# Wider steps of the crossbar: key tiles of 112, more transposes by DMA, and a new instruction order in a fused attention and FFT-convolution kernel

## The chip, the cores and the metric

The kernel runs on one core of a Trainium2 chip. A time is the device time of one execution in microseconds (us), as the median of several runs; a profile is one further execution, recorded instruction by instruction. PE is the matmul engine (PEld its weight loads), DVE the vector engine, ACT the scalar engine, POOL and SP the two engines that here mainly issue DMAs. PSUM is where PE writes, in banks that DVE and ACT empty.

## The reference

Local attention with a few global keys is followed by a gated long convolution:

```python
# q, k, v: (4 batches, 8 heads, 768 positions, 64), n_global 8, n_local 96
scores = (q @ k^T) / 8
keep   = (key < 8) | (0 <= query - key < 96)
scores += -slope[head] * distance        # 96 for a global key outside the local window
a = softmax(where(keep, scores, -1e9))
x = (a @ v), heads side by side          # (4, 768, 512)
x1, x2, x3 = split(x @ w_proj)           # w_proj (512, 1536)
x2 = irfft(rfft(x2) * rfft(filter))      # over the 768 positions
out = (x1 * x2 * x3) @ w_out             # float32
```

## The kernel before

Everything is fused, in float16 inside and float32 in PSUM. The four batches are software-pipelined: while one batch goes through the convolution, the next goes through attention.

*Attention* (`attention`, L855). The keys are cut into seven tiles of 120 local keys; with the 8 global keys in the first rows each fills 128 partitions (`KL = P - NG`, `K0`). A tile meets the 216 queries that can see it (`EW`), and the tiles go in groups `GRP` of 2, 2 and 3. For a group and each of four head pairs, `scores` (L685) runs the matmuls of the two heads on the two halves of the array, ACT takes the exponential from two banks into the tile `E` (L721), and DVE multiplies it by a mask that holds the distance bias (L738); in batch 0 the bias is added by extra matmuls in place of the mask. In `E` each tile's 216 columns stand 248 apart, with zeros in the gaps. `values` (L741) multiplies `E` by the values, whose column of ones gives the softmax sum; DVE takes the reciprocal (L785) and scales into `xn` (L780, or in small pieces on ACT, L784). Output tiles also step by 120 queries.

*Transposes.* q and k are loaded with positions on partitions by POOL's DMAs (L319), which convert to float16, into single buffers `qn` and `kn`. The matmuls need them transposed into `QT` and `KT`: batches 0 to 2 do it on PE (`turned`, L672) with a copy out of PSUM by DVE or ACT (L303), batch 3 (`XB`) by DMA transposes from the SP queue (`crossed`, L660). The attention output `xn` is transposed into `xT` on PE for all batches (`transpose_x`, L801), with a copy (L303). Copies of the global rows go from SP too (`kn<-kn`, `vn<-vn`).

*The rest* (`gate` L830, `butterfly` L808, `conv` L891). `gate` multiplies `xT` by the outer two thirds of `w_proj` (L840), evacuates x1 (L307 or L309) and x3 (L849), and multiplies them (L851). `butterfly` folds `xT` by sums and differences (tiles `xab`, `xcf`, `xo`, `xr`; L816 is its first step), so that the projection (L909, tile `ab`), the forward transform (L621, tile `X`), the products with the filter's spectrum, the inverse transform (L934, tile `eo`) and the recombination (`mix`, `half`, y*g) are short. L961 is the output projection, tile `ot` its evacuation, from which SP stores.

*What sets the order.* Each step is an operation in a list, with the engines that may run it, and what it reads and writes. `ORDER`, a string at the top, fixes the sequence of all of them: `33V` is operation 33 on DVE, `87P0` is operation 87 on PE with PSUM bank 0; A is ACT, G is POOL, S is SP. So the string also chooses between DVE and ACT where both are allowed ("AV"). Each engine runs its operations in this order and waits for what each reads:

```python
def crossed(self, what, ts, buf):
    ...
    x = g.op("S", 0.5, lambda _: nc.sync.dma_start_transpose(out=o, in_=i), ...
```

Of the kernel before, what the change touches and what calls it, by code (L numbers as in the profile page):

```python
# [18 lines left out]
KL = P - NG  # L19
# [7 lines left out]
def act(n):  # L27
    return 0.06 + n / 1200.0
# [11 lines left out]
5G 33V 34A 1V 16S 0V 12V 20S 4V 41A 43A 9V 8V 39A 10A 44A 36A 6A 49A 48A 19S 37A 45A 24G 17S 18S 50G 55G 25V 11V 26G  # L40
13V 56G 40A 42A 7V i14b0 87P0 54G 28A 53G 60G 31A 85P1 61G 59G 27A 72V 62G 52G 35A 81P2 51G 57G 46A 58G 83P3 47A 88A
29V 30V 32V 90P0 63G 89A 86A 82V 38A 91V 84A 21V 114P2 115V 94P01 98P45 116P2 78A 65G 99A 64G 15V 117V 95A 92P67 112P3
113V 93A 110P2 96P45 97A 158P3 66G 111V 122P01 123A 120P67 121A 22V 68G 159V 3G 160P3 161V 14V 23S 156P2 118P45 162P3
67G 119A 124P01 261G 157V 163V 164P23 125A 166P45 100P01 165A 101V 102V 167A 105P67 170P23 171A 69G 168P01 169A 131P45
262G 263G 106V 107V 108P2 132V 133V 260G 126P67 127V 76A 103P3 104A 109V 128V 75A 134P4 221P5 74A 135V 172P01 73A 173V
259G 129P6 216P4 177P23 79A 130V 136P6 174V 175P7 178V 70G 146P0 217A 264S 179V 180P1 137P2 222A 223V 142P3 176A 218V
219V 71G 80A 271G 202V 181A 183P1 182P4 203V 220A 224V 209V 144A 141P5 210V 138A 211V 148V 205V 361P3 273G 225A 139V
140V 272G 270G 265S 188P7 185A 362A 212V 213V 151P6 266G 363P3 2A 153V 143A 364V 359P2 360V 152P6 228P3 154V 276G
365P01 190A 184V 77A 204V 279G 366A 206V 207V 371P45 198P2 277G 226V 367V 155V 297P7 368P01 214V 372A 373V 215V 208V
200A 374P45 187P6 278G 229A 274G 145V 491G 298A 288P2 375A 269G 275G 369A 289A 488G 286P7 227V 235V 236V 189V 237V  # L50
147P4 149V 238V 287A 150V 230A 231A 232A 233V 284P2 285A 312P7 292P6 313A 293A 389P5 387P2 192P7 390A 194A 193P6 195A
388V 394P45 395A 400P01 234V 391P23 392A 239V 240V 376V 299P7 300A 437P6 401A 301P4 302A 282G 268S 433P5 435P7 438V
281G 370V 397P23 398A 241V 249P6 250A 393V 434V 247P4 436V 402V 267S 382P01 494S 242P5 248A 448P67 243A 439P23 493S
440A 383V 384V 449A 396V 303P4 377P01 197P5 199A 304A 399V 408P23 441V 492G 244P6 378V 379V 305P5 409V 410V 380P4
445P01 245A 442P23 280G 381V 306A 196V 446A 450V 403P67 404V 443A 411P5 489G 587P4 499G 405V 256P01 412A 490G 385P6
257A 505G 386A 258A 591P7 588V 252P45 253A 254A 507G 406P0 447V 456P23 661P1 444V 508G 501G 662A 407V 414P0 589P4 590A
251V 307V 416A 310P5 311A 511G 290P6 424P1 457V 458V 291A 426A 459P0 423P4 425A 429P6 308V 431A 500G 451P23 665P1
418P6 255V 592A 191V 615P4 314V 315V 506G 718G 309V 322P7 452V 246A 460A 502G 420A 453V 186V 323A 617P5 719G 454P0
455A 295V 294V 296V 732G 666V 318P6 721S 413P7 616A 330P0 316P2 509G 481V 482V 484V 317A 326P1 618A 415A 663P4 428P2
201V 430V 319A 320P3 321V 324P5 483V 325A 331V 328P7 327A 419P6 329A 421V 422V 495G 472P2 730G 664A 283G 734G 466P7  # L60
# [138 lines left out]
class Fused:  # L199
    PERIOD = 40.0  # L200
    NEAR = 3
    PAIR_X = ()
    PAIR_AB = ()
    PAIR_EO = ()
    PAIR_T = (1, 2, 3)
    PAIR_M = ()
    VD = 96
    XB = (3,)
    WL = [(0, 256), (1024, 256), (256, 256), (1280, 256), (512, 512)]
    SHIFT = 0.0  # L210
    LONG = 0.6
    EW = [216, 216, 216, 216, 216, 168, 48]
# [1011 lines left out]
```

## Time and profile before

| | us |
|---|---|
| median of 3 runs | 179.61 |
| lowest, highest run | 178.33, 181.84 |
| the profiled execution | 178.0 |
| its span, first to last instruction | 176.2 |
| PE, DVE, ACT, POOL busy in it | 163.8, 156.3, 148.7, 78.2 |
| granted PE clock | 1.00 |

The span is what the views divide up; the profiled execution's time holds 1.8 us around it. Busy time of an engine counts every instant at which one of its instructions ran; for PE, whose matmuls overlap, this is not the time that the work needs at least. A group's line gives the line of the code, engine, operation, output and input tiles, shapes, count, then busy time, the mean duration of one in ns, and the idle time of the engine just before it.

### The profile page before, as it was taken

What the parts mean: (1) busy time and instruction counts of PE and PEld (TensorE: products, weight loads), DVE (VectorE), ACT (ScalarE), POOL (GpSimd) and SP (SyncE); (2) the same over time, 40 slices, a digit from 0 to 9 for tenths busy, and PEclk for the clock granted to TensorE, in tenths of its full rate; (3) what the DMA queues carried; (4) which work ended last, traced back from release to release, by engine and by line L of the source; (5) the groups of instructions that cost most, each with busy time, mean ns of one, the idle gap of its engine ahead of it and who ended that gap; (6) DMA issues with size and microseconds to landing.
All of it is one profiled execution on the core that took longest, in us unless ns stands there. A gap on an engine that the chain in (4) does not pass through costs nothing.

```text
span 176.2 us, 4332 instructions
## 1 busy us (share of the span) xinstructions
PE 163.8 (93%) x1662; PEld 100.3 (57%) x1662; DVE 156.3 (89%) x339; ACT 148.7 (84%) x294; POOL 78.2 (44%) x99
## 2 busy tenths in 40 slices
PE   5989999689999999999899999999999999989981
PEld 2547976354655767654356767444676644556530
DVE  7685569869999999999999999999999999999960
ACT  6999998949999988889989999899856855957852
POOL 7999998828999468799950000000000000000000
PEclk9999999999999999999999999999999999999999
DMA  4999999999999989999999995400031030041564
GB/s 110 184 149 140 142 173 170 196 193 154 159 155 159 149 53 106 156 167 155 130 161 169 131 96 159 179 4 0 0 118 65 0 125 0 0 180 40 192 242 186
DMA packets 98188, 22.23 MB, mean 126 GB/s; under 512 B 90879, under 2 KB 95095, under 8 KB 98167
## 3 DMA queue, kind: packets, MB, share of 16 engines
q0 software_dynamic: 82992, 12.41, 98.6%
q1 hardware_dynamic: 15175, 9.54, 23.1%
q8 instruction: 13, 0.21, 0.5%
q14 instruction: 8, 0.07, 0.1%
HBM read 25.84 MB, written 6.29 MB: 182 GB/s over the span
## 4 chain that ended last, share of the span: by engine, by line
DVE 48%; PE 15%; POOL 11%; ACT 11%; issue 7%; DMA 6%; POOLq 0%; DVEq 0%; ACTq 0%; SPq 0%
DVE E L738 6%; PE bank L961 4%; DMA kn<-in_k_dram 4%; DVE xn L780 4%; DVE y L1041 4%; POOL vn L319 4%; DVE g L851 3%; DVE y L1036 3%; PE bank L840 3%; ACT E L721 3%; POOL kn L319 2%; DVE ab L309 2%; POOL qn L319 2%; ACT g L849 2%; DVE pp L1072 2%
## 5 line engine op out<-in xcount | busy, mean ns | idle before, releaser
L840 PE MATMUL bank<-xT,w 128*128 128x384 f16 x256 | 48.5, 326 | 0.2 <-DVE x L309 0.2
L721 ACT ACTIVATE E<-bank 128x864 f16<-128x864 f32 x48 | 40.7, 900 | 4.1 <-issue 2.2
L840 PEld LDWEIGHTS <-w 128*128 128x128 f16 x256 | 23.7, 98 | 16.1 <-issue 1.4
L319 POOL DMA_DIRECT2D kn<-in_k_dram x27 | 25.1, 935 | 6.3 <-DMA g<-in_moe_filter_fft_dram 2.7
L319 POOL DMA_DIRECT2D vn<-in_v_dram x28 | 25.5, 917 | 0.8 <-PE bank L761 0.8
L961 PE MATMUL bank<-wo,y 128*128 128x512 f16 x96 | 23.9, 379 | 1.1 <-DVE y L1041 1.1
L319 POOL DMA_DIRECT2D qn<-in_q_dram x21 | 18.9, 905 | 4.0 <-PE bank L621 3.9
L738 DVE TENSOR_TENSOR E<-E,mask 128x864 f16<-128x864 f16 x36 | 20.2, 599 | 0.0
L780 DVE TENSOR_TENSOR xn<-bank,rc 128x512 f16<-128x512 f32 (+1 forms) x22 | 16.9, 774 | 0.7
L756 PE MATMUL bank<-vn,E 128*128 128x65 f16 x224 | 15.5, 193 | 0.2 <-DVE xn L780 0.2
L307 ACT ACTIVATE ot<-bank 128x512 f32<-128x512 f32 x21 | 12.6, 620 | 3.7 <-PE bank L961 3.3
L756 PEld LDWEIGHTS <-E 128*128 128x128 f16 x224 | 14.0, 97 | 2.8 <-issue 0.8
L303 ACT CAST eo<-bank 128x384 f16<-128x384 f32 x28 | 12.3, 496 | 3.8 <-PE bank L937 3.7
L761 PE MATMUL bank<-vn,E 128*128 128x65 f16 x192 | 15.3, 193 | 0.0
L707 PE MATMUL bank<-QT,KT 64*128 64x216 f16 (+2 forms) x224 | 14.4, 241 | 0.8 <-DVE ab L309 0.3
L849 ACT CAST g<-bank 128x384 f16<-128x384 f32 x28 | 13.9, 502 | 1.5 <-PE bank L840 1.2
L961 PEld LDWEIGHTS <-y 128*128 128x128 f16 x96 | 8.8, 98 | 10.1 <-DVE y L1041 2.2
L303 ACT CAST X<-bank 128x512 f16<-128x512 f32 x24 | 13.6, 607 | 0.7 <-PE bank L621 0.7
L761 PEld LDWEIGHTS <-E 128*128 128x128 f16 x192 | 13.2, 97 | 1.0 <-issue 0.8
L307 ACT ACTIVATE x<-bank 128x384 f16<-128x384 f32 x23 | 11.4, 509 | 1.8 <-PE bank L840 1.0
L707 PEld LDWEIGHTS <-KT 64*128 64x128 f16 x224 | 8.3, 94 | 7.5 <-issue 4.6
L934 PE MATMUL bank<-inv,X 128*128 128x256 f16 x64 | 11.4, 273 | 1.1 <-DVE X L1078 1.1
(148 smaller groups left out, 348.3 us busy)
## 6 DMA issues: line engine op xcount, KB each, us to landing
out_dram<-ot SPq DMA_DIRECT2D x24, 256.0 KB
vn<-in_v_dram POOLq DMA_DIRECT2D x28, 120.0 KB, 5.6
kn<-in_k_dram POOLq DMA_DIRECT2D x27, 120.0 KB, 5.8
qn<-in_q_dram POOLq DMA_DIRECT2D x21, 128.0 KB, 5.9
w<-in_moe_w_proj_dram POOLq DMA_DIRECT2D x4, 256.0 KB, 6.8
ot<-in_q_dram SPq DMA_DIRECT2D x3, 256.0 KB
g<-in_moe_filter_fft_dram POOLq DMA_DIRECT2D x1, 768.0 KB, 11.4
w<-in_moe_w_proj_dram POOLq DMA_DIRECT2D x1, 512.0 KB, 8.7
```

The costliest lines, as they stand in the source:

```text
L303: {"A": nc.scalar.copy, "V": nc.vector.tensor_copy, "G": nc.gpsimd.tensor_copy}[e](out, in_)
L307: self.nc.scalar.mul(out, in_, c)
L319: return self.g.op(eng, 0.57 + 0.00035 * nbytes[0] if eng == "G" else 0.5, lambda _: e.dma_start(dst, src), w=w, r=r, nbytes=nbytes, name= ...
L707: nc.tensor.matmul(bs[hh].f32()[:, off:off + w], self.KT[hs, hp, P * m:P * m + P], self.QT[hs, hp, KL * m:KL * m + w], start=(off == 0 and ...
L721: g.op("A", act(864), lambda _: nc.scalar.activation(eo, bs[0].two()[:, :, 0:432].rearrange("p h (m w) -> p h m w", m=2), Act.Exp, scale=s ...
L738: g.op("V", dve(864, 2), lambda _: nc.vector.tensor_mul(eo, eo, mk), r=[("mask", 2 * hp), ("mask", 2 * hp + 1)], w=[("E", hp, gi)], name=" ...
L756: nc.tensor.matmul(o[:, n, hh], ef[:, at:at + P], vt[:, t, 2 * hp + hh, 0:D + 1], start=first, stop=(t == 0), skip_group_check=True)
L761: nc.tensor.matmul(o[:, n, hh], ef[:, at:at + P], vt[:, t - 1, 2 * hp + hh, 0:D + 1], start=False, stop=True, skip_group_check=True)
L780: nc.vector.tensor_mul(to, o[:, :, :, 0:D], rc.to_broadcast([P, 2, 2 * nt, D]))
L840: nc.tensor.matmul(bk.f32()[:, 0:h], self.w[:, c, o + P * j:o + P * j + P], self.xT[:, c, h * s:h * s + h], start=(c == 0), stop=(c == 3))
L849: first = g.op("AV", {"A": act(h), "V": 0.0005}, lambda e: nc.scalar.copy(x3, pts[1].f32()[:, 0:h]) if e == "A" else None, use=[pts[1]], w ...
L961: nc.tensor.matmul(bk.f32(), y[:, c, P * t:P * t + P], self.wo[:, c, :], start=(c == 0), stop=(c == 3))
```

## The change

- **Key tiles of 112.** A key tile holds 112 local keys; rows 0 to 7 are the global keys, rows 8 to 15 are padding (zeros in k, zeros loaded once into v by two DMAs, masked in the bias). A tile meets 208 queries, the last one 96. Output tiles step by 112. Group widths in the exponential become 416, 416 and 512 per head.
- **No gaps in `E`.** The columns of a group are contiguous; the value matmul with the previous key tile takes its remaining 96 columns and writes 96 output rows.
- **Crossbar.** `XB` becomes (2, 3): q and k of batch 2 as well as 3 go by DMA transpose. For batches 2 and 3 (`XX`) the attention output goes through it too (`crossed_x`: one DMA of up to 112 partitions by 512 for each tile, seven a batch), in place of `transpose_x`. `xn` becomes one tile for this, with the four head pairs side by side.
- **Set-up.** Slopes are written by 8 wider instructions in place of 16; the fills of `E` shrink to one.
- **Order.** `ORDER` is another sequence, with other choices between DVE and ACT. `PAIR_M`, which was empty, goes.

```diff
-KL = P - NG
+KL = 112
+LO = P - KL
...
-5G 33V 34A 1V 16S 0V 12V 20S 4V 41A 43A 9V 8V 39A 10A 44A 36A 6A 49A 48A 19S 37A 45A 24G 17S 18S 50G 55G 25V 11V 26G
...
-1021S 1022P4 1023A 1016P5 1024S 1017A 1018S
+0V 15S 1V 18S 32V 10V 5G 23G 2A 39A 36A 35A 34A 33A 6V 7V 41G 16S 9V 24V 26V 44G 25G 8V 47G 37A 45G 46G 40A 51G i14b0
...
+994P7 995A 996S
...
-    PAIR_M = ()
...
-    XB = (3,)
+    XB = (2, 3)
...
-    EW = [216, 216, 216, 216, 216, 168, 48]
+    N, LAST = 208, 96
+    EW = [208] * 6 + [96]
+    GW = [416, 416, 512]
...
-    Q0 = [0, 240, 480]
-    QW = [240, 240, 288]
+    Q0 = [0, 224, 448]
+    QW = [224, 224, 320]
+    XX = (2, 3)
...
-        self.EE = t("E", [P, 4, 2, 1536])
+        self.EE = t("E", [P, 4, 2, 1376])
...
-        self.mask = t("mask", [P, H, 648])
-        self.xn = [t(f"xn{i}", [P, 2, 7, 2, D]) for i in range(2)]
+        self.mask = t("mask", [P, H, 720])
+        self.xn = t("xn", [P, 7, 4, 2, D])
...
-        g.op("V", dve(512, 2), lambda _: v.memset(self.ot[3][0:NG], 0.0), w=[("kz", 0)], bias=-4500)
-        for lo, hi in ((1, 2), (2, 7)):
-            g.op("V", dve(512 * (hi - lo), 4), lambda _, lo=lo, hi=hi: v.memset(self.kn[0:NG, lo:hi], 0.0),
-                 w=[("kz", t) for t in range(lo, hi)], bias=-4500 if lo == 1 else -3500)
-        for i in range(4):
-            et = self.E[i]
-
-            def gaps(e, et=et):
-                gap = et[:, :, 0:1488].rearrange("p h (m w) -> p h m w", m=6)[:, :, :, 216:248]
-                if e == "V":
-                    v.memset(gap, 0.0)
-                    v.memset(et[:, :, 1456:1536], 1.0)
-                    return
-                zero = self.idle[:, 0:384].rearrange("p (h m w) -> p h m w", h=2, m=6)
-                nc.scalar.copy(gap, zero)
-                nc.scalar.activation(et[:, :, 1456:1536], self.idle[:, 0:160].rearrange(
-                    "p (h w) -> p h w", h=2), Act.Copy, bias=1.0, scale=1.0)
-            g.op("AV", {"A": 0.62, "V": 0.52}, gaps, r=["idle"], w=[("E", i, c) for c in range(3)], name="gaps")
+        g.op("V", dve(512), lambda _: v.memset(self.ot[3][0:LO], 0.0), w=["kz32"], name="kz")
+        for lo, hi in ((0, 2), (2, 7)):
+            g.op("V", dve(512 * (hi - lo), 2), lambda _, lo=lo, hi=hi: v.memset(self.kn[0:LO, lo:hi], 0.0),
+                 w=[("kz", t) for t in range(lo, hi)], name="kz")
+        g.op("V", dve(256), lambda _: v.memset(self.EE[:, :, :, 1344:1376], 1.0),
+             w=[("E", i, c) for i in range(4) for c in range(3)], name="gaps")
...
-                dst = self.slope[ps, hp].rearrange("p k c -> p (k c)")
-                dst = dst[:, 0:256].rearrange("p (k c) -> p k c", k=2)
-                for k in range(2):
-                    g.op("A", {"A": 0.145}, lambda e, ps=ps, hp=hp, k=k: self.times(
-                        e, self.slope[ps, hp, k, 64 * k:64 * k + 64], self.ident[ps, ps],
-                        self.slopes[2 * hp + ps.start // 64] / self.scale),
-                        r=["ident", "slope"], w=[("slope", half, hp, k)], bias=-2950, name="slope")
+                at = 1024 + 256 * hp
+                dst = flat[ps, at:at + 384].bitcast(BF16).rearrange("p (k c) -> p k c", k=2)[:, :, 0:64]
+                g.op("A", {"A": 0.32}, lambda e, ps=ps, hp=hp, dst=dst: self.times(
+                    e, dst, self.ident[ps, None, ps].to_broadcast([64, 2, 64]),
+                    self.slopes[2 * hp + ps.start // 64] / self.scale),
+                    r=["ident", "slope"], w=[("slope", half, hp, k) for k in range(2)], name="slope")
...
-        g, nc, NL, n = self.g, self.nc, self.NL, 216
+        g, nc, NL, n = self.g, self.nc, self.NL, self.N
...
-            for lo, hi, at in ((0, n, 0), (0, n, n), (0, 168, 2 * n), (n, n + 48, 600)):
-                v.tensor_copy(wide[:, at:at + hi - lo], dg[:, lo:hi])
+            v.tensor_copy(wide[:, 0:2 * n].rearrange("p (a b) -> p a b", a=2),
+                          dg[:, None, 0:n].to_broadcast([P, 2, n]))
+            v.tensor_copy(wide[:, 2 * n:3 * n + self.LAST], dg)
...
-        g.op("V", 0.9, spread, r=["dg", "far"], w=["wide"], name="spread")
+        g.op("V", 1.35, spread, r=["dg", "far"], w=["wide"], name="spread")
...
-            g.op("A", act(648), lambda _, h=h: nc.scalar.activation(
+            g.op("A", act(720), lambda _, h=h: nc.scalar.activation(
...
-        x = g.op("S", 0.5, lambda _: nc.sync.dma_start_transpose(out=o, in_=i), nbytes=(128 * n, 1024),
+        g.op("S", 1.25, lambda _: nc.sync.dma_start_transpose(out=o, in_=i), nbytes=(128 * n, 1024),
...
-        x.svc = 2.0 * n
...
-        g.op("P", 0.555 if near else 0.19 if gi == 2 else 0.187, run, acq=bs, r=[("QT", t) for t in qt] + [
+        g.op("P", (0.54, 0.55, 0.65)[gi] if near else (0.182, 0.182, 0.222)[gi], run, acq=bs, r=[("QT", t) for t in qt] + [
...
-        eo = et[:, :, 496 * gi:496 * gi + 496].rearrange("p h (m w) -> p h m w", m=2)
-        eo = eo[:, :, :, 0:216]
-        g.op("A", act(864), lambda _: nc.scalar.activation(
-            eo, bs[0].two()[:, :, 0:432].rearrange("p h (m w) -> p h m w", m=2), Act.Exp,
-            scale=self.scale), use=bs, w=[("E", hp, gi)], table="exp", name="exp")
+        W = self.GW[gi]
+        eo = et[:, :, 416 * gi:416 * gi + W]
+        g.op("A", act(2 * W), lambda _: nc.scalar.activation(
+            eo, bs[0].two()[:, :, 0:W], Act.Exp, scale=self.scale), use=bs, w=[("E", hp, gi)],
+            table="exp", name="exp")
...
-        if (self.b, gi) in self.PAIR_M:
-            if hp % 2:
-                hs = slice(2 * hp - 2, 2 * hp + 2)
-                ep = self.EE[:, hp - 1:hp + 1].rearrange("p a h c -> p (a h) c")[
-                    :, :, 496 * gi:496 * gi + 496].rearrange("p h (m w) -> p h m w", m=2)[:, :, :, 0:216]
-                mk = self.mask[:, hs].rearrange("p h (m w) -> p h m w", m=3)
-                mk = (mk[:, :, 0:2], mk[:, :, 1:2].to_broadcast([P, 4, 2, 216]), mk[:, :, 1:3])[gi]
-                g.op("V", dve(1728, 2), lambda _: nc.vector.tensor_mul(ep, ep, mk),
-                     r=[("mask", h) for h in range(hs.start, hs.stop)], w=[("E", hp - 1, gi), ("E", hp, gi)], name="masked")
-            return
-        mk = self.mask[:, 2 * hp:2 * hp + 2].rearrange("p h (m w) -> p h m w", m=3)
-        mk = (mk[:, :, 0:2], mk[:, :, 1:2].to_broadcast([P, 2, 2, 216]), mk[:, :, 1:3])[gi]
-        g.op("V", dve(864, 2), lambda _: nc.vector.tensor_mul(eo, eo, mk),
+        mo = (0, self.N, self.N)[gi]
+        mk = self.mask[:, 2 * hp:2 * hp + 2, mo:mo + W]
+        g.op("V", dve(2 * W, 2), lambda _: nc.vector.tensor_mul(eo, eo, mk),
...
-                        at = 248 * t if t < 6 else 248 * 5 + 168
+                        at = self.N * t
...
-                            at = 248 * (t - 1) + KL
-                            nc.tensor.matmul(o[:, n, hh], ef[:, at:at + P],
+                            at = self.N * (t - 1) + KL
+                            nc.tensor.matmul(o[0:self.LAST, n, hh], ef[:, at:at + self.LAST],
...
-        vs = [("vn", slot, t) for t in range(max(0, ts[0] - 1), ts[-1] + 1)] + [("vn1", slot)] + [
+        vs = [("vn", slot, t) for t in range(max(0, ts[0] - 1), ts[-1] + 1)] + [("vn1", slot), ("vz", slot)] + [
...
-            to = self.xn[j][:, :, ts[0]:ts[0] + nt].rearrange("p i t h d -> p i (t h) d")
+            to = self.xn[:, ts[0]:ts[0] + nt, 2 * j:2 * j + 2].rearrange("p t i h d -> p i t h d")
...
-                nc.vector.tensor_mul(to, o[:, :, :, 0:D], rc.to_broadcast([P, 2, 2 * nt, D]))
+                nc.vector.tensor_mul(to, o[:, :, :, 0:D].rearrange("p i (t h) d -> p i t h d", h=2),
+                                     rc.rearrange("p i (t h) o -> p i t h o", h=2).to_broadcast([P, 2, nt, 2, D]))
...
-                    nc.scalar.mul(to[:, i, n], o[:, i, n, 0:D], rc[:, i, n])
+                    nc.scalar.mul(to[:, i, n // 2, n % 2], o[:, i, n, 0:D], rc[:, i, n])
...
-                    nc.tensor.transpose(tx[:, o:o + P], self.xn[j][:, i, t], self.ident)
+                    nc.tensor.transpose(tx[:, o:o + P], self.xn[:, t, 2 * j + i], self.ident)
...
+
+    def crossed_x(self, c, t):
+        n = min(KL, self.S - KL * t)
+        o, i = self.xT[:, :, KL * t:KL * t + n], self.xn[0:n, t].rearrange("p a h d -> p (a h d)")
+        self.g.op("S", 1.25, lambda _: self.nc.sync.dma_start_transpose(out=o, in_=i), nbytes=(n, 1024),
+                  r=[("xn", j, c) for j in range(2)], w=[("xT", j, c) for j in range(2)], name="cross")
...
-                self.transpose_x(j, c)
+                if b not in self.XX:
+                    self.transpose_x(j, c)
+            for t in self.GRP[c] if b in self.XX else ():
+                self.crossed_x(c, t)
...
-            self.g.op("V", 0.36, ones, w=[("vn1", i)], name="ones", bias=at)
+            self.g.op("V", 0.45, ones, w=[("vn1", i)], name="ones", bias=at)
...
-        for what, o, src, t, p0 in (("q", 0, self.q, 0, 0), ("k", 3, self.k, 0, NG), ("q", 1, self.q, 1, 0),
+        for i in range(2):
+            pad = self.vn[i][NG:LO].rearrange("p t h d -> p (t h d)").rearrange("p (a b) -> p a b", a=12)
+            zero = self.idle[NG:LO, None, 0:448].to_broadcast([LO - NG, 12, 448])
+            self.load("S", pad, zero, [("vz", i)], (96, 896), "vz", r=["idle", ("vn1", i)])
+        for what, o, src, t, p0 in (("q", 0, self.q, 0, 0), ("k", 3, self.k, 0, LO), ("q", 1, self.q, 1, 0),
```

## The prediction

> **What bounds the kernel now.** I read the page's first two parts, then busy time by stretch, then the groups of instructions kept apart by shape, then the SyncE queue's own timeline.
>
> ```profile
> PE 163.8 (93%) x1662; PEld 100.3 (57%) x1662; DVE 156.3 (89%) x339; ACT 148.7 (84%) x294; POOL 78.2 (44%) x99
> DVE  7685569869999999999999999999999999999960
> DMA  4999999999999989999999995400031030041564
> ```
>
> ```profile
> 0.00:40.00 40.00, 35.04 (x441) 23.07 (x442) 29.12 (x83) 34.66 (x68) 34.07 (x51) 1.00 1.69 162
> 40.00:170.00 130.00, 126.44 (x1212) 76.36 (x1210) 127.05 (x257) 112.20 (x224) 44.08 (x49) 1.00 1.11 109
> 140.00:150.00 10.00, 9.95 (x55) 5.04 (x54) 9.83 (x19) 5.75 (x13) 0.00 (x0) 1.00 0.14 55
> 170.00:176.20 6.20, 2.33 (x10) 0.90 (x10) 0.15 (x1) 1.85 (x4) 0.00 (x0) 1.00 0.65 251
> ```
>
> The columns are length, then PE, PEld, DVE, ACT and POOL busy, the clock and DMA. In the 130 us from 40 to 170 PE is busy 97%, DVE 98%, ACT 86%; together 365.7 of 390, a mean share of 93.8%. No engine alone is the bound: work taken off one is a gain only as far as the others are relieved or can take over. ACT's slack lies after 130 (5.75 of 10 at 140). Ahead of 40 loads and set-up pace the kernel; after 170 the last stores.
>
> ```profile
> L738 DVE TENSOR_TENSOR E<-E,mask 128x864 f16<-128x864 f16 x36 | 20.2, 599 | 0.0
> L780 DVE TENSOR_TENSOR xn<-bank,rc 128x512 f16<-128x512 f32 x15 | 10.3, 690 | 0.4
> L309 DVE TENSOR_SCALAR x<-bank 128x384 f16<-128x384 f32 x9 | 5.0, 551 | 0.2
> L309 DVE TENSOR_SCALAR ab<-bank 128x512 f16<-128x512 f32 x6 | 4.1, 682 | 0.0
> L307 ACT ACTIVATE ab<-bank 128x512 f16<-128x512 f32 x18 | 11.0, 622 | 1.7 <-PE bank L909 1.5
> L784 ACT ACTIVATE xn<-bank,rc 128x64 f16<-128x64 f32 x20 | 4.3, 340 | 0.2 <-DVE rc L785 0.2
> L303 ACT COPY xT<-bank 128x480 f16<-128x480 f16 x10 | 5.6, 566 | 2.3 <-PE bank L801 2.2
> L303 ACT COPY KT<-bank 128x1024 f16<-128x1024 f16 x4 | 4.1, 1031 | 0.0
> ```
>
> ```profile
> 12.45 8.41 ACT L721 ACTIVATE E<-bank 128x864 f16<-128x864 f32 x10 [0.35 <-PE bank L707]
> 30.89 2.62 DMA kn<-kn
> 99.25 0.45 PE bank L801 x8
> 137.91 0.96 DVE xab L816
> ```
>
> ```profile
> L660 SPq DMA_TRANSPOSE KT<-kn x7: 1188/1258/1879, 82.9 to 105.3; - x7
> L660 SPq DMA_TRANSPOSE QT<-qn x6: 1190/1254/1937, 85.4 to 102.0; - x6
> 85.44 4.78 SPq L660 DMA_TRANSPOSE QT<-qn  x2
> ```
>
> The last fence is the crossbar as batch 3 uses it already: 13 crossings of one 128x512 tile, 1.25 us of the SP queue each in the middle, 1.94 at most; two once took 4.78 us together. Copying the first rows of kn inside SBUF by DMA landed after 2.62 us, my nearest row for a landing.
>
> **The change, part by part.** The order names an engine for each operation by a letter, so I counted the letters of both orders by kind. Prices are busy time over count, or the slope between two sizes.
>
> *PE.* Gone are the transposes of q and k of batch 2 (13 tiles x 4) and of x in batches 2 and 3 (2 x 28): 108, at 0.45 us for eight, 6.05 us. Added are 48 score columns per head pair and batch (group widths 432, 432, 432 become 416, 416, 512) and twice that for batch 0's bias: 0.5 us at 0.42 ns a column (four 384-column matmuls take 0.65 us). Net -5.5. The value matmuls keep their number; 96 for 128 rows in some I put at nothing (they follow one another 0.03 us apart).
>
> *DVE.* Evacuations move to ACT: x1 9 to 2 (7 x 0.56 = -3.9), ab 6 to 1 (5 x 0.68 = -3.4), xn of 512 15 to 13 (-1.4), eo, g from PSUM and inv one each (-1.0). QT and KT copies of 1024 fall 5 to 3 (-1.4), xT 8 to 6 (-0.8). Added: one X copy (0.6), two mix scalings (0.7), and the mask products: 36 at 0.517 back to back (1.55 us for three) become 24 of 832 and 12 of 1024 elements, at 0.52 ns an element 19.2 for 18.6 us (0.6). The fills of the E gaps in set-up fall by 0.9, one small negation adds 0.3. Net -10.6.
>
> *ACT.* Added: x1 23 to 30 (+3.5), x3 and eo one each (+0.9), ab 18 to 23 (+3.1), xn in small pieces 20 to 36 (16 x 0.215 = +3.4), inv (+0.4), eight masks of 720 for 648 (+0.5). An exp back to back is 0.841 us (8.41 for ten); with 0.86 ns an element (from copies of 512 and 1024) 32 of 832 and 16 of 1024 make 41.7 for 40.4 (+1.3). That the exps now write without gaps I price at nothing, since these ten ran gapped at the same slope. Gone: xT 16 to 6 (-6.0), copies of 1024 5 to 2 (-3.1) and three of 512 (-1.8), mix scalings (-1.7), slopes 16 to 8 larger ones, small fills and an X copy (-3.5). Net -3.0, of which -2.5 in set-up.
>
> *SP and DMA.* 27 crossings more, 40 in all, in one queue with the stores. Their price lies between 1.25 us (the median) and 2.39 (the pair of 4.78); I take 1.25, near eleven of thirteen rows: 50 us of a queue that has some 80 between batch 2's first loads and batch 3's last values. Behind a crossing that waits on xn stand others and two copies of vn; behind the last of batch 2's x stands its butterfly. For batch 3 the new order leaves DVE six products, two sums, three gates, a y product and two ot (8.65 us by their rows) between the last xn and that butterfly, for four crossings and a landing: 4 x 1.25 + 2.62 = 7.6 us, hidden. At 2.39 each it would be 12.2, 3.5 us late. I take 0.4 us lost in all, between 0 and 12.
>
> [...]
>
> *Loads and set-up.* Tiles of 112 rows send fewer packets; descriptor work does not show it (kn of 120 rows 935 ns, qn of 128 905), so nothing, 1 us at best, on a POOL idle after 92. Set-up: its savings stand beside waits for loads; I take nothing, between -2 (batch 1's first k tile stands earlier in the queue, and 30 to 40 has 2.3 us of idle PE) and +1.
>
> *Sum.* Within 40 to 170 the three engines lose 5.5 + 10 + 0.5 = 16 us of work. At the same mean share that is 16 / 3 / 0.938 = 5.7 us; PE alone gives the same, 5.5 / 0.973. Less 0.4 for crossings: -5.3. The span goes from 176.2 to 170.9, the profiled execution's 178.0 to 172.7. The median shown is 1.6 above that execution, so the forecast is **174.3**.
>
> **Rivals.** *The relief does not come through.* The new order could leave each engine waiting for another where each now waits 2 to 3%; at a mean share of 91% in place of 93.8 the stretch takes (365.7 - 16) / 3 / 0.91 = 128.1, so only 1.9 us are won: 177.7. For it: every operation's place is new. Against it: the work is truly gone. Chance 0.23.
>
> *DVE was the bound.* The chain that ended last is 48% DVE; if it alone sets the pace, 10 / 0.977 = 10.2 us go: 169.4. Against it: PE at 97% must then work without gaps. Chance 0.12.
>
> *The crossbar queue becomes the bound* (slower). 40 crossings at 2.39 us are 95.6; begun at about 48 us (SP's first copy of batch 2's kn rows is issued at 51.11 now), the last x tile lands near 146.2 and not at 137.9, where batch 3's butterfly starts now. With the 38.3 us that follow it today the span is 184.5: 187.9 in the median's terms. It decides from about 2.1 us a crossing on, or when one queued crossing waits long for a load. For it: loads run beside batch 2's crossings all the time (the DMA row stands at 9 until slice 24) and x crossings wait for xn in order with those of batch 3's q and k. Against it: eleven of thirteen rows were short with the loads running. Chance 0.15. [...]
>
> *No relief in work and no loss*: the order gives back just what it saves, 179.6; chance 0.07.
>
> **How the numbers follow.** The forecast itself has 0.43. A measurement of this kernel tells about 2% from no change: 176.0 and 183.2 are the limits. Below 176.0 lie nearly all of the forecast, the DVE case and a little of the first rival: 0.59. Within lie the rest of that rival, the equal case and the mild end of the crossbar case: 0.28. Slower: 0.13. The range reaches from the DVE case with a us to spare, 168.5, to the limit 183.0, leaving most of the crossbar case out.
>
> **What would show it.** Right: PE some 5 us and DVE some 10 us less busy, ACT within 3 us of now, all three at the same share from 40 to the tail; 40 crossings at a median near 1.3 us; no idle time of DVE ahead of batch 3's butterfly, that of L816's line. Wrong: crossings near 2 us, PE or DVE waiting on them by name or as unexplained issue time, the SP queue still crossing at 140 us, or DVE idle although its work fell.

## The result and the profile after

| | before | after |
|---|---|---|
| median (runs) | 180.4 us (4) | 186.25 us (4) |
| lowest to highest | 178.33 to 181.84 | 185.97 to 188.02 |
| profiled span | 176.2 us | 184.4 us |
| granted PE clock in it | 1.00 | 0.952 |
| PE, DVE, ACT busy | 163.8, 156.3, 148.7 | 165.1, 145.3, 146.7 |

The kernel became slower: the ratio is 1.043, with an interval of 1.030 to 1.055. A ratio, here and below, leaves out slow runs (of before those of 181.19 and 181.84 us), so it is not the quotient of the medians. The forecast was 174.3 us and its range ended at 183.0.

The first two parts of the page after, and its DMA queues; the lines of before stand in the prediction. The columns of the queues are packets, MB, and the packets' time as a share of 16 engines' span; q0 carries POOL's loads, q1 what SP issues: stores, copies, and the transposes by DMA, which are called crossings here.

```profile
PE 165.1 (90%) x1556; PEld 102.4 (56%) x1556; DVE 145.3 (79%) x317; ACT 146.7 (80%) x295; POOL 73.2 (40%) x99
...
PE   7999399999999999989905999969999999999991
...
DVE  7664053999999999989900899859998999999940
...
PEclk9999955899999999999985999999999999999999
DMA  5999999999999999999999943646021472001376
...
q0 software_dynamic: 75952, 11.95, 92.4%
q1 hardware_dynamic: 28984, 12.98, 32.2%
```

The work fell as counted: DVE is 11.0 us less busy, ACT 2.0. PE's busy time did not fall, but part of it ran at half clock (the fives in the PEclk row), and there the same work is slower: near 25 us two value matmuls, a pair, start every 0.13 us, where a pair takes 0.077 at full clock (140.09 to 140.63 us, seven pairs). What is new are holes: PE has a slice of 3 and a slice of 0, and DVE falls to 0 at both places. The DMA row stands at 9 from the second slice to slice 23. That row looked almost the same before (9 to slice 24); the experiments below lead back to it.

The stretch for which the forecast was made (length, then PE, PEld, DVE, ACT and POOL busy, clock, DMA) and the crossings in SP's queue (duration in ns, shortest, median, longest, and first and last start):

```profile
40.00:170.00 130.00, 119.31 (x1098) 72.32 (x1096) 114.94 (x231) 108.54 (x229) 41.00 (x49) 0.97 1.20 122
```

```profile
L651 SPq DMA_TRANSPOSE KT<-kn x14: 1203/1272/2497, 57.3 to 122.4; - x14
```

```profile
L651 SPq DMA_TRANSPOSE QT<-qn x12: 1205/1260/1672, 55.0 to 116.2; - x12
```

```profile
L793 SPq DMA_TRANSPOSE xT<-xn x14: 1184/1210/2036, 104.3 to 145.8; - x14
```

The mean share of the three engines is 342.8 of 390, or 87.9%, where it was 93.8. The crossings cost the queue what they cost it before.

What the holes wait for, first from the waits of after (us in total, times, longest), then from its chain (start, length, what):

```profile
PE bank L737 <- DMA vn<-vn: 7.1, 1, 7.1
POOL kn L321 <- DMA KT<-kn: 7.0, 1, 7.0
```

```profile
14.17 8.36 DMA vn<-idle
...
71.00 8.26 DMA KT<-kn
...
86.57 4.99 DMA vn<-in_v_dram
92.06 6.85 DMA vn<-vn
```

The first hole is the fill of v's padding rows, a DMA that the new order issues at 14.17 us and that lands 8.36 us later. At 71 us a crossing of a k tile takes 8.26 us to land; POOL's next load of k needs that tile's place in `kn`, and batch 2's loads of v stand behind it in POOL's order. They come late, the copy of their global rows comes later still, and PE stands still until 99 us.

The stretches in which the clock was halved (length, then busy PE, PEld, DVE, ACT, POOL, clock, DMA):

```profile
24.00:33.00 9.00, 9.00 (x108) 7.50 (x105) 4.49 (x12) 4.93 (x8) 8.43 (x11) 0.50 1.77 162
...
96.00:102.00 6.00, 2.95 (x31) 2.26 (x32) 0.86 (x4) 0.48 (x3) 1.06 (x2) 0.50 1.83 156
```

Each follows a hole, of 3.0 and 7.1 us. So the profile offers four suspects: two transfers that stand badly in their queues, the clock, the single buffer `kn`, and the DMA engines themselves.

### The profile page after: what moved, and what is told of

Its sections match the earlier page's. It is cut to its first block, busy times and chain, and to the rows that moved or that the text cites. A ratio compares the mean times of both kernels' runs of the same rounds, so it can differ in the third digit from the quotient of the medians.

```text
span 184.4 us, 4173 instructions
## 1 busy us (share of the span) xinstructions
PE 165.1 (90%) x1556; PEld 102.4 (56%) x1556; DVE 145.3 (79%) x317; ACT 146.7 (80%) x295; POOL 73.2 (40%) x99
## 3 DMA queue, kind: packets, MB, share of 16 engines
q0 software_dynamic: 75952, 11.95, 92.4%
## 4 chain that ended last, share of the span: by engine, by line
PE 69%; DMA 16%; DVE 4%; issue 3%; POOL 3%; SPq 2%; ACT 1%; DVEq 0%; POOLq 0%
PE bank L828 15%; PE bank L900 12%; PE bank L952 8%; PE bank L612 6%; PE bank L742 6%; PE bank L737 5%; DMA vn<-idle 5%; DMA KT<-kn 4%; DMA vn<-vn 4%; PE bank L698 4%; PE bank L301 3%; DMA vn<-in_v_dram 3%; PE bank L925 2%; PE bank L662 2%; PE bank L783 2%
## 5 line engine op out<-in xcount | busy, mean ns | idle before, releaser
L712 ACT ACTIVATE E<-bank 128x832 f16<-128x832 f32 (+1 forms) x48 | 41.9, 942 | 3.6 <-PE bank L698 3.6
L737 PE MATMUL bank<-vn,E 128*128 128x65 f16 x224 | 21.3, 210 | 10.0 <-DMA vn<-vn 7.1
L737 PEld LDWEIGHTS <-E 128*128 128x128 f16 x224 | 19.7, 120 | 12.7 <-issue 8.3
L719 DVE TENSOR_TENSOR E<-E,mask 128x832 f16<-128x832 f16 (+1 forms) x36 | 21.4, 614 | 0.0
L742 PE MATMUL bank<-vn,E 128*96 128x65 f16 x192 | 21.4, 224 | 0.0
L767 DVE RECIPROCAL rc<-bank 128x8 f32<-128x8 f32 (+1 forms) x24 | 4.9, 209 | 20.3 <-PE bank L742 19.9
L742 PEld LDWEIGHTS <-E 128*96 128x96 f16 x192 | 19.8, 143 | 0.8
L309 ACT ACTIVATE ab<-bank 128x512 f16<-128x512 f32 x23 | 13.8, 635 | 4.4 <-PE bank L900 4.3
L698 PE MATMUL bank<-QT,KT 64*128 64x208 f16 (+1 forms) x224 | 14.6, 247 | 1.4 <-DMA KT<-kn 0.8
L766 ACT ACTIVATE xn<-bank,rc 128x64 f16<-128x64 f32 x36 | 7.8, 335 | 8.9 <-DVE rc L767 8.8
```

The source lines that it names most:

```text
L309: self.nc.scalar.mul(out, in_, c)
L698: nc.tensor.matmul(bs[hh].f32()[:, off:off + w], self.KT[hs, hp, P * m:P * m + P], self.QT[hs, hp, KL * m:KL * m + w], start=(off == 0 and ...
L712: g.op("A", act(2 * W), lambda _: nc.scalar.activation(eo, bs[0].two()[:, :, 0:W], Act.Exp, scale=self.scale), use=bs, w=[("E", hp, gi)], ...
L719: g.op("V", dve(2 * W, 2), lambda _: nc.vector.tensor_mul(eo, eo, mk), r=[("mask", 2 * hp), ("mask", 2 * hp + 1)], w=[("E", hp, gi)], name ...
L737: nc.tensor.matmul(o[:, n, hh], ef[:, at:at + P], vt[:, t, 2 * hp + hh, 0:D + 1], start=first, stop=(t == 0), skip_group_check=True)
L742: nc.tensor.matmul(o[0:self.LAST, n, hh], ef[:, at:at + self.LAST], vt[:, t - 1, 2 * hp + hh, 0:D + 1], start=False, stop=True, skip_group ...
```

## The experiments

The kernel before was run again beside each group of experiments, with medians between 177.95 and 178.52 us. Ratios are against those.

### Single waits taken away

**The fill of the padding ahead** (`11V` and `13S`, two places in `ORDER`):

```diff
-0V 15S 1V 18S ... 16S 9V ... 4V 11V 87P67 ... 262G 13S 148V
+0V 15S 1V 11V 18S ... 16S 13S 9V ... 4V 87P67 ... 262G 148V
```

> The changed kernel with the first zero fill of v's padding rows (vn<-idle) issued at about 3 us in place of 14.2, so that it lands long before the first value matmuls; nothing else moves. Place in the queue (theory): the 3.0 us in which PE waits for it from 19.6 on, and the half clock from 23.7 to 33.6 behind it, are gone; the clock is 1.00 until 92; 4 to 6 us less than the changed kernel, about 181. Rival, slow landings under load: v itself lands late, PE still waits 1 to 3 us there for in_v, and no more than 2 us are won. Rival, a bad order everywhere: under 1 us.

**The copy of batch 2's first global rows of v directly behind the other copy** (`487S`):

```diff
-468P6 488S 344P4 ... 661A 487S 329V
+468P6 488S 487S 344P4 ... 661A 329V
```

> The changed kernel with the copy of batch 2's global rows into the first two v tiles (vn<-vn) issued directly behind the copy into the other five, at about 77 us, in place of 92.06; nothing else moves. Place in the queue: the wait of 7.1 us from 92 on and the half clock from 95.4 to 102 are gone; 6 to 9 us less than the changed kernel, about 178 to 180. Rival, slow landings under load: the values then wait for in_v (tile 1 is issued at 86.6 and lands some 5 us later) or for a crossing, and 3 us or less are won. Rival, a bad order everywhere: under 1 us.

**Both moves**:

> Both moves together. Place in the queue: the sum of both, 11 to 14 us less than the changed kernel, 172 to 175, a clock of 1.00 throughout, and thus 2 to 5% faster than before: the forecast's 174.3 was right but for two copies in a queue. Rival, slow landings under load: 178 to 182, with PE or DVE waiting for crossings or in_v instead. Rival, a bad order everywhere: 184 or more.

**PE kept busy in both holes** by matmuls of zeros, to see whether the clock then stays up:

```diff
-91P67 ... 595P23
+i12b6 91P67 ... i30b2 595P23
```

> The changed kernel with matmuls on zeros put ahead of the two late groups of value matmuls (12 of 512 columns at 19.6 us, 30 at 92 us), which PE runs while it waits; their results are used by nobody. The waits stay, but PE is never idle there. If the granted clock falls because PE stood idle, it stays at 1.00 and 3 to 6 us are won, about 181: that is the clock's part of the loss, and the rest is the waits themselves. If the clock falls for another reason (the instructions that come then, or DMA load), the half clock is still there and nothing is won.

Measured: 185.55 us (ratio 1.040, 1.030 to 1.049), 185.61 (1.030, 1.017 to 1.043), 184.81 (1.033, 1.025 to 1.042) and 185.42 (1.038, 1.025 to 1.050). The first three took away the waits that they aimed at, the fourth the early half clock; none brought the time back, and all four intervals overlap that of the changed kernel. With both moves the waits and the chain read:

```profile
POOL kn L321 <- DMA KT<-kn: 16.1, 2, 10.0
PEld L698 <- DMA KT<-kn: 12.3, 4, 6.3
```

```profile
56.72 12.55 DMA kn<-in_k_dram
69.29 10.46 DMA KT<-kn
96.09 7.23 DMA KT<-kn
122.45 2.43 DMA KT<-kn
```

What the early fill wins by 40 us is lost again between 55 and 110 us. A load of k lands after 12.55 us (5.8 in the median of before), a crossing behind it after 10.46, another after 7.23; when the loads are over, the crossing at 122 us lands in 2.43. The theory that two transfers merely stood in the wrong place fell here. So did the early half clock as the cause: the run with busy matmuls has a clock of 1.00 from 23 to 34 us and is as slow. Its clock fell later: the PEclk row reads 5 from 78.4 to 83.0 us. PE's own row falls first, to 5 in the slice from 73.8 us, where the clock still reads 9, and the longest new wait of PE is one of 4.9 us for `KT<-kn`; so the idle time came first there.

### The buffer, or the engines behind it

**`kn` as a ring of nine tiles**, so that a load waits for the crossing two tiles further back (with both moves):

```diff
-        self.kn = t("kn", [P, 7, H, D])
+        self.kn = t("kn", [P, 9, H, D])
+    def slot(self, b, t):
+        return (7 * b + t) % 9
```

> All 40 crossings and both early moves, but kn is a ring of nine tiles in place of seven, so that a load of k waits for the crossing two tiles further back; crossings, loads, and their order are the same. Theory: POOL's waits for DMA KT<-kn fall from 16 us to under 5, the loads of batch 2 and 3 are issued some 8 us earlier, and 184.8 falls to 179 to 182. Rival 3 (not the buffers but the 16 DMA engines: the crossings get their turn late beside the loads, and PE waits on KT and QT for that): POOL's waits fall but PE's and the weight loads' waits for KT (some 21 us together by name) do not, and the time stays at 183.5 to 185.5.

Measured 185.4 us (1.038, 1.030 to 1.046). POOL's wait for `KT<-kn` is gone; PE's waits for it are shorter but remain, and one for `QT<-qn` has come (L705 is the line of the score matmuls here):

```profile
PEld L705 <- DMA KT<-kn: 8.4, 3, 5.5
PE bank L705 <- DMA KT<-kn: 7.7, 2, 5.3
POOL qn L321 <- DMA QT<-qn: 6.6, 1, 6.6
```

The loads no longer wait for k's buffer, and the crossings land no sooner (9.73 and 7.54 us in the chain, for 10.46 and 7.23). The theory of k's buffer fell as well; the rival that names the DMA engines gave the number. The buffer of q stayed as it was, and POOL now waits for it.

### Parts undone in the changed kernel

**q and k of batch 2 on PE again, in the order of after, and the same with both moves** (`XB = (3,)`; the transposes and their copies, on DVE, were put into `ORDER` by hand):

> Only batch 3's q and k cross (13 crossings); batch 2's 13 tiles are transposed on PE again and copied out by DVE (8 groups more, some 2.9 us of PE and 6 us of DVE); x of batches 2 and 3 still crosses, and the rest of the new order stands. Theory (the crossings of q and k of batch 2, which land in 5 to 10 us beside the loads, hold the single buffers kn and qn, so that POOL's loads behind them start late): POOL's wait for DMA KT<-kn before 85 us falls from 7 to 0, the last load is issued by 92 us in place of 97; the two stalls of PE at 20 and 92 us are not touched, unless the second shrinks since the loads are earlier; 186.25 becomes 181 to 184. Rival 1 (the new order or the 112-key tiles as such cost the time): 186 to 190, as PE and DVE get work back. Rival 2 (x's crossings cost it): 186 to 189.

> The same, with the fill of the padding and the copy of batch 2's global v rows moved ahead, so that neither of PE's two long stalls should be there. Theory: what was won by these two moves is no longer given back between 60 and 110 us; granted clock above 0.985, 177 to 180, against 184.8 for the two moves alone. Rivals 1 and 2: 184 to 187, with waits of PE and DVE elsewhere (rival 2: for DMA xT<-xn, more than the 1.3 us of the kernel after).

**x on PE again** (`XX = ()`, with both moves):

> The opposite half: q and k of batches 2 and 3 cross (26 crossings), x of all batches is transposed on PE again (56 transposes more, 3.2 us of PE, and 12 copies, six on DVE and six on ACT, 3.3 us each); with both early moves. Theory (q and k's crossings hold the buffers): POOL still waits some 16 us for DMA KT<-kn, and the time is 184 to 188. Rival 2 (x's crossings cost the time): POOL may wait as before but the time falls to 178 to 181.

**q and k of all batches on PE, x crossing** (`XB = ()`, with both moves):

> The kernel after with both early moves and with q and k of all batches on PE (26 tiles, 104 transposes, some 5.9 us of PE and 16 copies on DVE, some 10 us); only x of batches 2 and 3 crosses (14 crossings, begun when the loads are over). Both theories: no wait of PE for KT or QT crossings is left, the granted clock stays at 1.00, and PE's busy time is some 168 us at 94 to 95% of the span: 176 to 180. Rival (the new order or the 112-key tiles cost time by themselves): 183 or more, with the idle time in other places.

Measured: 185.61 (1.042, 1.038 to 1.047), 182.65 (1.029, 1.021 to 1.037), 191.67 (1.076, 1.072 to 1.081), 184.16 (1.034, 1.024 to 1.043). Without the 13 crossings of batch 2, and with both moves, the median is 2.2 us below that with them, although PE has 2.9 us of work back; that is the sign that the suspicion asks for, but the intervals overlap (1.021 to 1.037 and 1.025 to 1.042) and settle nothing; it lies between the theory's 177 to 180 and the rivals' 184 to 187. Taking x's crossings away made the kernel slower, above even the 184 to 188 that was expected, so they show no sign of being the culprit. But the four kernels were not as clean as meant. In the last one the clock is at 0.998 and nobody waits for a crossing, and still it takes 184 us; both theories had expected 176 to 180, and 183 or more was the mark of the rival that the new order or the 112-key tiles cost time by themselves. Its waits:

```profile
POOL kn L321 <- PE bank L662: 8.7, 2, 5.3
...
DVE QT L305 <- PE bank L662: 5.2, 8, 1.2
```

The transposes that I put in by hand make POOL and DVE wait for PE. So the runs neither bear that rival out nor remove it; the kernel with fewer loads, below, speaks to it. The next ones alter the kernel before.

### One part done alone in the kernel before

**Batch 2's q and k cross, in the places where PE transposed them:**

```diff
-    XB = (3,)
+    XB = (2, 3)
```

> The kernel before with one part of the change alone: batch 2's q and k cross (13 crossings in the places where PE transposed them), nothing else is changed; 52 transposes and 8 copies less. Theory B: the work falls by 2.9 us on PE and some 6 us on ACT and DVE, but PE's scores of batch 2 and POOL's loads of batch 3 wait for landings of 5 to 10 us beside the loads; 181 to 186, with PE's waits for KT and QT by name over 5 us. Theory A: as slow, but then with the extra crossings of the other kernel as slow too. If crossing them were free, the time would be 174 to 176.

Measured 184.07 us (1.032, 1.025 to 1.038). This one part takes away 52 transposes and eight copies and costs 5.7 us or so (3.2% of 178). Its waits:

```profile
POOL qn L319 <- DMA QT<-qn: 10.4, 1, 10.4
...
POOL kn L319 <- DMA KT<-kn: 5.4, 1, 5.4
```

Here too crossings hold buffers, and the loads move less: from 74 to 94 us q0 carried 2.06 MB and not 2.56. This run does not tell the two apart.

### Crossings that nobody waits for

**Thirteen extra crossings in the kernel before**, of tiles of QT and KT into an unused output buffer, beside the loads:

> The kernel before with 13 crossings more of a 128x512 tile, from columns of QT and KT that batch 2 has just got, into an unused output buffer: nobody waits for them and they hold no load buffer. They are issued while the loads still run (some 70 to 80 us). Theory A (crossings take so much of the 16 DMA engines from the loads that they cost time even if nobody needs them): the loads of batch 3 land some 5 us later, 178 becomes 181 to 185. Theory B (it is the late landing of crossings that someone waits for): 178 to 180, as before within its scatter; at most the 13 real crossings of batch 3 behind them in the queue start later.

Measured 195.82 us (1.084, 1.074 to 1.094), but it is no measure of contention: the crossings waited for one another's four destinations, ACT waited 16.0 us for one of them, and the copies of vn's global rows stood behind them in SP's queue, so that PE waited 18.2 us for `vn<-vn`. The next two were meant to mend this: six crossings of zeros, each with a destination of its own, where the queue is free.

```diff
+    def extra(self, n):
+        to = ...
+        self.nc.sync.dma_start_transpose(out=to.rearrange("p (a b) -> p a b", a=4), in_=self.idle)
```

**Beside the loads:**

> The kernel before with six more crossings of a 128x512 tile of zeros into output buffers that are unused then, issued at some 74.7 to 82.2 us, where its SP queue is free and the loads of batches 2 and 3 run; nobody waits for them and the queue's next crossing is due at 82.9. Theory A (a crossing takes its share of the DMA engines from the loads, near 1 us of the load stream each by the run with 13): loads land later, POOL's last load is issued some 5 us after 90.6, 178 becomes 180 to 183. Theory B (only a landing that someone waits for costs time): 177.5 to 178.7.

**After them:**

> The control: the kernel before with the same six extra crossings behind its first six stores, from some 107 us on, when the loads are over. Both theories: 177.5 to 178.7, no difference.

Measured: 183.12 us (1.024, 1.016 to 1.033) beside the loads; 179.17 (1.003, 0.998 to 1.007) after them. Here is what the two queues moved from 74 to 94 us, in the kernel before, then with the six crossings beside the loads:

```profile
q0 software_dynamic: 19341, 2.56, 200.5%
q1 hardware_dynamic: 1697, 0.51, 18.8%
```

```profile
q0 software_dynamic: 11539, 1.85, 144.2%
q1 hardware_dynamic: 3916, 1.04, 49.1%
```

In the same 20 us the loads on q0 moved 0.71 MB less (0.86 less than the control, which moved 2.71 there). At 2.56 MB in 20 us that is 5.5 to 6.7 us of the load stream, some 0.9 to 1.1 us for each crossing. In bytes it is 0.12 to 0.14 MB for each, and a tile of 128x512 float16 holds 0.13: a crossing displaced about its own size in loads. POOL's own timeline shows the same (start, length, then the idle time before it and what ended it):

```profile
85.60 0.89 POOL L328 DMA_DIRECT2D qn<-in_q_dram  x1 [1.77 <-DMA vn<-in_v_dram]
...
91.83 0.90 POOL L328 DMA_DIRECT2D vn<-in_v_dram  x1 [1.64 <-DMA vn<-in_v_dram]
```

By this view POOL now waits, 0.3 to 1.8 us each time, until earlier loads of other tiles have landed before it issues the next. Its last load is issued at 97.8 us and not at 89.7. From 105 to 115 us PE is busy 6.88 of 10 us, where it was 9.70. PE waits there for crossings of batch 3's q and then of its k, by the waits (us in total, times, longest) and the chain (start, length, what):

```profile
PE bank L716 <- DMA QT<-qn: 2.8, 1, 2.8
```

```profile
105.00 4.94 DMA KT<-kn
```

This crossing of k was issued at 95.81 us before. Both stand in SP's queue behind two crossings of q that hold it for 9.90 us from 88.81 us on (4.78 before, 2.0 of them a wait for a load of q); loads of q land there in 11.2 us in the median from 74 to 94 us, and in 5.7 before. The queue has a part of its own, too: the six took 10.8 us of it and not 7.5 (six times 1.25), so batch 3's first crossing began 4.2 us late, at 87.07 us. In the control no crossing of batch 3 stands behind the extra ones. So the pair of runs shows that crossings delay loads; how much of the 5 us came that way, and how much through SP's queue, it does not tell.

### The stream of loads made lighter

**The 14 loads of v of batches 2 and 3 left out**, in the changed kernel with both moves and all 40 crossings, and in the kernel before as a control:

```diff
-            self.load_rows(("vn", s), vt, self.v, b, t)
+            if b >= 2:
+                self.g.op("G", 0.1, lambda _: None, w=[("vn", s, t)], name="left out")
+            else:
+                self.load_rows(("vn", s), vt, self.v, b, t)
```

> The changed kernel with both early moves (184.8) and all its 40 crossings; only the 14 loads of v of batches 2 and 3 are left out (1.7 MB; batches 2 and 3 are computed with the v that lies in the buffers, so the output is not the reference's). Theory A (crossings and loads share the DMA engines, and the stream of loads and crossings together is what is late): 14 loads less are some 12 us of the stream, crossings land sooner, PE's waits for KT and QT between 55 and 110 us and POOL's waits for crossings shrink to under 5 us, and the time falls to 174 to 178. Rival (the changed kernel loses its time in the order of its instructions on PE, DVE and ACT): 182 to 185.

> The control: the kernel before without the same 14 loads. Its engines are 93 to 98% busy between 40 and 170 us, so a lighter stream of loads can win it little: 176.5 to 178. With both at that, the difference between the two kernels is the stream and no more; with the changed kernel below it by 2% or more, the work that the change saves comes out as time once the stream is light.

Measured: the changed kernel falls from 184.81 to 175.16 us (0.980, 0.973 to 0.988, so just under 2% below before), the kernel before stays at 178.4 (1.002, 0.998 to 1.007). The same loads are worth 9.7 us to the one and nothing to the other. The page of the changed kernel without them:

```profile
PE 158.6 (92%) x1556; PEld 97.8 (57%) x1556; DVE 145.4 (84%) x317; ACT 146.9 (85%) x295; POOL 61.8 (36%) x85
...
PEclk9999999999999999999999999999999999999998
```

At full clock PE is 5.2 us less busy than before, near the 5.5 of the forecast. The new order and the 112-key tiles, with all crossings, thus run below the kernel before when the loads are fewer, which speaks against the rival that they cost the time by themselves. One part of the expectation missed: POOL still waits 13.0 us for `KT<-kn`. That wait did little harm here, with 14 loads fewer behind it: the time was 175.16 us with it. Leaving the loads out lightens the DMA engines and shortens POOL's queue at once (q0 carries 10.34 MB and not 11.95, POOL is busy 61.8 us and not 73.3), so this pair shows that the stream of loads was late, and not which of the two delays it most.

### Weights of 96 columns

In the full-clock run with x alone crossing, weight loads read (count, busy, mean ns):

```profile
L737 PEld LDWEIGHTS <-E 128*128 128x128 f16 x224 | 16.6, 108 | 1.8
L742 PEld LDWEIGHTS <-E 128*96 128x96 f16 x192 | 16.4, 126 | 0.6
```

Before, both lines had 128 columns and 97 ns; the second read:

```profile
L761 PEld LDWEIGHTS <-E 128*128 128x128 f16 x192 | 13.2, 97 | 1.0 <-issue 0.8
```

There two value matmuls followed each other in 0.062 us; here a pair takes an estimated 0.0785, and 0.077 in the timeline of the changed kernel near 140 us.

**The kernel before with 96 columns:**

```diff
-                            nc.tensor.matmul(o[:, n, hh], ef[:, at:at + P],
+                            nc.tensor.matmul(o[0:96, n, hh], ef[:, at:at + 96],
```

> The kernel before, except that its value matmuls with the previous key tile (192 of them) take 96 columns of E in place of 96 and 32 zeros, as the kernel after does. If a weight load of 96 columns is slower than one of 128 (126 to 97 ns in the traces), each such pair takes 0.0785 us for 0.062, PE is 3.2 us busier, and with PE at 93% the time is 180 to 181.5 for 178; if it is free (as the prediction took it), 177.5 to 178.5.

**The x-only kernel with 128:**

> The kernel in which only x crosses, with 128 columns of E in place of 96 in the value matmuls with the previous key tile. The 32 columns more are those of the next tile's first queries, so the sums of 16 rows of each output tile contain terms that they should not; it is for the time alone. If the 96-column load is what costs: PE's busy time falls by 3 us and 184.2 becomes 181 to 182. If not: 183.5 to 184.5.

Measured: 179.24 us (1.002, 0.997 to 1.007) and 183.19 (1.029, 1.020 to 1.036; 184.16 with 96 columns). With 128 columns the second weight load is back at 98 ns, and PE is 2.1 us less busy (164.7 for 166.8) where 192 pairs by 0.0165 us make 3.2 (2.9 by the 0.015 of the timeline). In the time of the kernel before nothing of it is seen. For the x-only kernel the two intervals overlap; whether it gains is open.

## Why the prediction was wrong, point by point

**The work terms came out near.** DVE -11.0 for -10.6, ACT -2.0 for -3.0, and PE -5.2 for -5.5 where the clock was full (-4.4 against the control without the same loads, 163.0). For PE luck has a part: the 96 columns, which the prediction "put at nothing", cost some 2 us of PE, so the rest of PE's work fell by about that much more than the sum has it. POOL's issue of a k load, put at nothing as well, fell from 935 to 836 ns with the smaller tiles; no run isolates what that is worth.

**"At the same mean share" did not hold, even with light loads.** There, from 40 to 166 us, PE, DVE and ACT are busy 119.92, 116.49 and 108.81 us, a mean share of 91.3%; the control keeps 93.8% from 40 to 170. That 175.16 us lies near 174.3 is luck in part: the kernel before stood at 178.5 beside it and not at 179.6, so 3.4 us were won where the forecast had 5.3.

**The step that failed is the one under "SP and DMA".** It priced a crossing by the SP queue: 1.25 us of issue, with 2.39 as the upper bound. That price was right: the medians of after lie between 1.21 and 1.27 us. But SP was not what ran short. By the runs it was the stream of loads beside the crossings: the DMA row stands at 9 to slice 23, six added crossings took 0.71 to 0.86 MB from it in 20 us, and with 14 loads fewer the changed kernel took 175.16 us. The sum has no term for it. The row of 9s to slice 24 was quoted and served only to ask whether crossings would be issued slowly. A crossing took 0.9 to 1.1 us of the load stream in the run with six, so the 13 of batch 2 that stand beside loads are an estimated 12 to 14 us of it. From 55 to 97 us the two queues moved this, before and then after:

```profile
q0 software_dynamic: 37371, 4.96, 182.1%
q1 hardware_dynamic: 2988, 0.85, 14.1%
```

```profile
q0 software_dynamic: 28334, 4.03, 153.9%
q1 hardware_dynamic: 9424, 2.40, 46.1%
```

The loads moved 0.93 MB less there; over the whole span they are only 0.46 MB smaller (11.95 for 12.41).

**The landing was mis-sized.** 2.62 us, from a copy of `kn` rows, fits the crossings after the loads: 2.4 us for xT with both moves, issued from 99.7 to 144.6 us. Beside loads they took 7 to 10.5 us in the chains above.

**Waits that the change adds were not named.** A load of batch 3's k or q now waits until a crossing of batch 2 has landed and no longer for a transpose on PE; behind it on POOL stand the loads of v. And the fill of the padding rows, counted with set-up at nothing, took 8.36 us to land, 3.0 of them on PE's path. Moving the fill and the copy of v's global rows ahead brought the ratio from 1.043 to no less than 1.030, since other waits, for crossings and loads, set the pace after them.

**"I take 0.4 us lost in all, between 0 and 12"** reached almost to the loss: 186.25 less 173.9, the forecast without its 0.4, is 12.35. The value taken was the wrong end. It was chosen by rows of issue, and the doubt that loads run beside batch 2's crossings was left to a rival with a chance of 0.15.

**The rivals.** "The crossbar queue becomes the bound" gave 187.9 us, near the result, by another mechanism: in the changed kernel crossings did not become slower in the queue. Its last clause, a queued crossing that waits long for a load, is nearer to what happened. "The relief does not come through" named a loss of mean share without a cause: 91% for the 87.9 of after, so that its 177.7 fell short, but close to the 91.3 with light loads.

**The signs it named.** PE, DVE and ACT waited by name for crossings and for transfers behind them, and DVE fell idle although its work fell: both were listed as "wrong". SP was still crossing at 145.8 us, but for x of batch 3, and no wait for one of these exceeds 0.7 us. The one idle time ahead of a butterfly was in batch 2, 2.6 us.

**What stays open.** That crossings and loads delay one another is shown by bytes and landings; that a late stream of loads is what the changed kernel loses by, by leaving loads out. How the loss divides among the DMA engines' time, the buffers that crossings hold, and SP's queue was not told apart, and undoing batch 2's crossings in the changed kernel gave no gain clear of noise. No kernel with the whole computation beat the one before; the best of the changed ones took 182.65 us. How much the 112-key tiles, the gapless exps and x's crossings are worth by themselves is not known either, since the variants that isolate them were ordered by hand.

## What to carry to other kernels

Before a transpose moves from PE to the crossbar, look at the DMA row where the crossing will stand, not at the queue that issues it: in this case, where the row was full, the crossings were paid for by the loads, about byte for byte (0.12 to 0.14 MB for a tile of 0.13), and the place to look for the price was when the last load is issued and lands. Here an engine with little slack (PE busy 97% from 40 to 170 us) and a DMA row at 9 stood side by side, and 52 transposes taken off PE for 13 crossings cost 5.7 us. To test such a thing cheaply, add the transfer where nobody waits for it, or leave other transfers out, with the kernel before as the control for both; and look what stands behind the added transfer in its own queue.

## What the runs showed of the hardware that was not expected

- **Crossings displaced loads.** With six crossings added from another queue, the loads moved 1.85 MB in 20 us, where they moved 2.56 in the kernel before and 2.71 in the control. The crossings got through, and both sides landed later (2.4 to some 10 us for a crossing, 5.8 to 12.55 for a load of k). How the engines divide their time between the two queues, no run here shows.
- **Half clock for long after a short hole.** In the changed kernel PE was idle for 3.0 us, and then ran at 0.50 from 24 to 33 us although it was busy 9.00 of these 9 us. After the hole of 7.1 us it ran at 0.50 from 96 to 102 us, busy 2.95 of these 6, and at 0.98 from 102 to 104. What sets these lengths was not isolated. Keeping the clock at 1.00 over the first stretch won no time clear of noise (185.42 us for 186.25).
- **Weights of 96 columns loaded slower than those of 128**: 126 ns in the run with x alone crossing, 97 in the kernel before, and 98 once the x-only kernel took 128. The rows do not show why.
- **A small fill landed late.** Eight partitions of zeros, 84 KB, took 8.36 us to land beside loads (issued at 14.17 us in the changed kernel).
